# Scores in the up projection's two banks, six raw blocks ahead, embeddings later, and 256 instead of 512 tokens' down projection in float32

## The chip, the cores and the metric

The kernel runs on one core of a Trainium2 chip. The metric is the device time of one execution in microseconds; the median of three runs of the kernel before is 1092.6 us (1091.49 to 1093.6). Five engines work side by side, each through its own queue in order: PE (TensorE, matmuls), DVE (VectorE), ACT (ScalarE), POOL (GpSimd) and SP (SyncE, here the queue of most DMA issues).

## The reference

Three stages follow each other, on float64 inputs for w_in and w_out and float32 for most else:

```
attention, B=8 batches, H=8 heads, S=512 tokens, Ns=32 states, D=64:
  scores  = x @ state^T / 8 ; a = softmax(scores) ; xread = a @ state
  scores2 = state @ x^T / 8 ; a2 = softmax(scores2) ; sread = a2 @ x
  out = concat(xread, sread) -> 4608 tokens x 512
moe:   h = x @ w_in (512 x 2048) ; g = relu(h)^2 ; y = g @ w_out (2048 x 512)
moe2:  logits = normalize(y) @ normalize(expert_emb)^T / tau
       expert = argmax ; gate = softmax(logits)[expert], 8 experts
       out = gate * (relu(y @ w1[expert]) @ w2[expert])      (512 -> 1024 -> 512)
```

## The kernel before

The kernel is one program without loops on the chip. Python generators (`attention`, `block`, `up1`, `down1`, `embeddings`, ...) stand for threads of work; a `Plan` runs them against a clock of its own. Each `yield "engine", duration` asks for an engine, and the planner always issues the piece that can start first by its clock (`dep`, `free`), and among equals the one with the smaller priority number. A `yield ev(...)` waits for an event, a `yield slots` for a free buffer. What it issues in that order is each engine's queue on the chip, so the planner's durations set the order of work, not its time.

*Weights.* w_in and w_out are each read in eight raw blocks of 1 MB (i0 to i7 and o0 to o7, in the order i0 i1 o0 o1 i2 i3 ...). `weights()` asks for them one after another; `AHEAD` says from which block on it waits until both transposes of the first batch's attention weights have been asked for (events "asked"). A raw block becomes float32 in `to_f32` (an ACT conversion at L903, a cast at L910 on ACT or L913 on DVE, and an or on DVE at L916), is squared for its scale (L935 and L991 on ACT), and is later split into a high and a low float16 half: w_in in `wi_split` (L978), w_out in `wo_split` (L1039 on ACT, then DVE in `split_lo`, L317). The halves of w_out's block q go where the float32 copy of block q - 2 lies, so the split of block q waits for the float32 matmuls that read block q - 2: `yield ev("down32", F32U - 1, q - 2)`.

*Attention folded into the up projection.* The read xread @ w_in is computed as a @ (state @ w_in). For each batch, state @ w_in is made in four pieces k = 0 to 3 (events ("sw", b, k)): for the first batch in float32 from the float32 blocks of w_in (`first_state_w`, PE at L650, scaled and split at L660 and L317), for the others in float16. The S tile in PSUM (`ps_s`, two banks, one slot `s_slots`) holds these pieces, and also the scores of a batch.

*The first batch.* `first_attention` scores x in float32 in two halves t = 0, 1 (`first_scores`, L598); `weigher` makes the softmax (L520 maximum, L522 subtraction, L529 exponential, L531 sum, L537 division, L541 and L543 the two float16 halves) and asks for a transpose (L550). In the kernel before both halves lie in one S tile.

*Token groups.* The 4608 tokens are taken in groups u of 256, two groups a batch, u = 16 for all states. `up1` makes the hidden layer in eight chunks of 256 columns for each group (L1379 to L1381, three float16 matmuls for a product), `hidden` applies relu (L1332) and the square, and `down1` makes the output of each tile of 128 tokens. For the groups u < F32U the square stays float32 (L1336) and the down projection is done in float32 from the unsplit w_out (L1442). For the others the square is split in a high and a low half (L1344 or L1349, L1346, L1351) and the down projection takes three float16 matmuls (L1463 to L1465), which need the splits of w_out (`ev("wo", a)` in the first such group). With F32U = 2, `up1` alternates chunks of u = 0 and u = 1 as the pieces of state @ w_in come. From u = 2 on, chunk c of a group waits for part c - 1 of the down projection before it.

*Embeddings and constants.* `embeddings` loads the expert embeddings, tau and the float16 constants through ACT's DMA queue and normalizes the embeddings with 22 short DVE instructions (itau at L1166, the root at L308 to L314, the rest at L1183 to L1189) and four matmuls (L1174). `prepare` loads the other constants through SP and writes a row of records; its event "prepared" opens `down1`. The routing of each output tile (`route_tile`) waits for the embeddings (event "en").

Behind the first stage the experts' weights are converted, records of tokens are written to DRAM, and `moe2` works through lists of tokens by expert until the end.

Of the kernel before, what the change touches and what calls it, by code (L numbers as in the profile page):

```python
# [10 lines left out]
F32 = mybir.dt.float32  # L11
# [10 lines left out]
B, H, S, D, NS = 8, 8, 512, 64, 32  # L22
# [21 lines left out]
BLOCKS = [(kind, 2 * k + i) for k in range(NB // 2) for kind in "io" for i in range(2)]  # L44
RAW_IN = ('g0', 'g2', 'stage0', 'stage1', 'g1', 'g3', 'phl', 'wo8', 'stage0', 'stage1', 'phl', 'wo8', 'stage0', 'stage1',
          'phl', 'stage0')
F32U = 2
PRIO_W = 1
PRIO_SPLIT = 1.3
EASE = 1.0  # L50
LOADER = 9
AHEAD = 4
PRIO_A0 = 0.8
PRIO_A1 = 1.5
PRIO_S0 = 1.1
# [190 lines left out]
def moe_kernel(  # L246
# [17 lines left out]
    nc = tc.nc  # L264
    ctx.enter_context(tc.manual_schedule())
    plan = Plan()
# [70 lines left out]
    def load(dst, src, nbytes):  # L337
        yield "sp", 0.06
        nc.sync.dma_start(dst, src)
        return plan.dma(nbytes)  # L340
# [60 lines left out]
    def ev(*key):  # L401
        return evs.setdefault(key, Ev(plan))
# [46 lines left out]
    def attention(b):  # L449
# [50 lines left out]
        for sb in range(4):  # L500
            for c in range(4):
                o = Sp[:, sb, c * 64:c * 64 + 64]
                ss_ = slice(sb * 128, sb * 128 + 128)
                for n, (a, w) in enumerate(pairs):
                    mm(o, lhsT=w[:, c, ss_], rhs=a[:, c, :], start=n == 0, stop=n == 2)
        w = weigher(b, Sp, xh, xl, scl, 0, 32)
        yield from w

    def weigher(b, Sp, xh, xl, scl, m0, m1):

        ms, n = slice(m0, m1), NS * (m1 - m0)
        S4 = Sp.rearrange("p a (h n) -> p (a h) n", n=NS)[:, ms]
        mx = small.tile([128, 32], F32, name="mx")[:, ms]
        e1 = xh.rearrange("p c s -> p (c s)").bitcast(F32).rearrange("p (m n) -> p m n", n=NS)
        a16 = xl.rearrange("p c s -> p (c s)").rearrange("p (t c m n) -> p t m c n", t=2, c=4, n=NS)
# [5 lines left out]
        yield dve(n)  # L521
        V.tensor_tensor(out=e1, in0=S4, in1=mx.unsqueeze(2).to_broadcast([128, m1 - m0, NS]), op=ALU.subtract)  # L522
        ev("S read", b, m1).set()
        if m1 == 32:
            if m0:
                yield ev("S read", b, m0)
            s_slots.release()
        yield act(n)
        nc.scalar.activation(out=e1, in_=e1, func=AF.Exp, scale=scl)  # L529
        yield dve(n)  # L530
# [30 lines left out]
    def first_attention():  # L561

        yield ev("st", 0)
        stt = st_t.pop(0)
        yield xhl_slots
        xh, xl = halves_tile()
        ss = small.tile([128, 3], F32, name="ss")
        yield act(256)
        nc.scalar.activation(out=xl.bitcast(BF16)[:, :, :64], in_=stt, func=AF.Square, accum_out=ss[:, 2:3])
        yield t_slots  # L570
        p = ps_t.tile([128, 512], F32, name="t")
        yield "pe", 0.2
        mm(p[:, 2:3], lhsT=one32, rhs=ss[:, 2:3], start=True, stop=True)
        mm(p[:, 256:512], lhsT=oneb, rhs=xl.bitcast(BF16)[:, :, :64], start=True, stop=True)
        yield s_slots
        Sp = ps_s.tile([128, 4, 256], F32, name="S")
        for t in range(2):
            plan.add(first_scores(t, Sp, xh, xl, stt), 0.4 + 0.1 * t)
        plan.add(first_scale(ss, stt), 0.95)
        v = small.tile([128, 2], F32, name="sv")[:, 0:1]  # L580
        yield tiny(4)
        V.tensor_scalar(out=v, in0=p[:, 2:3], scalar1=FLOOR, scalar2=None, op0=ALU.max)
        pow2(sx[:, 1:2], isx[:, 1:2], v, 204)
        yield sth_slots
        sthl = att.tile([128, 2, 4, 64], F16, name="sthl")
        stf = sthl.rearrange("p a c n -> p (a c n)").bitcast(F32).rearrange("p (c n) -> p c n", c=4)
        yield dve2(256)
        V.tensor_scalar(out=stf, in0=stt, scalar1=sx[:, 1:2], scalar2=float(2.0 ** -14), op0=ALU.mult, op1=ALU.mult)
        plan.add(first_state_w(stf), 0.6)
        plan.add(group_bound(0, p), 0.7)  # L590

    def first_scores(t, Sp, xh, xl, stt):
        yield ev("first x", t)
        xf = xf_t[0, 0]
        yield "pe", 2.0
        for sb in (2 * t, 2 * t + 1):
            for c in range(4):
                mm(Sp[:, sb, c * 64:c * 64 + 64], lhsT=xf[:, c, sb * 128:sb * 128 + 128], rhs=stt[:, c, :],  # L598
                   start=True, stop=True)
        ev("scored", t).set()  # L600
        yield from weigher(0, Sp, xh, xl, eighth, 16 * t, 16 * t + 16)

    def first_scale(ss, stt):

# [551 lines left out]
        ev("experts").set()  # L1156

    def embeddings():
        yield "act", 1.0
        nc.scalar.dma_start(emf, embT)  # L1160
        nc.scalar.dma_start(tsb, tau.to_broadcast([128, 1]))
        nc.scalar.dma_start(cs16, cst16)
        plan.cur[2] += 2.5
        ev("identb").set()
        yield tiny(3)
        V.reciprocal(out=itau, in_=tsb)  # L1166
        V.tensor_scalar(out=itau, in0=itau, scalar1=float(2.0 ** -14), scalar2=None, op0=ALU.mult)
# [679 lines left out]
    def prepare():  # L1847

        yield ev("w_in asked")
        yield from load(cs, cst, 1 << 17)  # L1850
        yield from load(rid, rowid, 1 << 15)
        t = plan.now()
        yield "pool", 1.0, t + 2.0
        dz = mg.tile([128, REC], F32, name="rec0", bufs=1)
        nc.gpsimd.memset(dz, 0.0)
        nc.gpsimd.tensor_copy(dz[:, 513:514].bitcast(I32), rid[:, NT:NT + 1])
        yield from load(rec_d[NOREC:NOREC + 1, :], dz[0:1, :].bitcast(I32), 2048)
        ev("prepared").set()

    def start():  # L1860
        plan.add(first_attention(), PRIO_A0)
        yield from load_st(0)
        yield from load_x(0, 0)
        plan.add(embeddings(), 0.9)
        yield from block(0)
        plan.add(weights(), 1)
        for b in range(1, B):
            plan.add(attention(b), 1.15 if b == 1 else PRIO_A1)
        plan.add(loader(), 1)
        plan.add(prepare(), 1)  # L1870
        plan.add(up1(), 5)
        plan.add(down1(), 5)
        plan.add(moe2(0, NMAIN), 5)
        plan.add(switch(), 2.1)
# [46 lines left out]
```

## Time and profile before

| | us |
|---|---|
| median of 3 runs | 1092.6 |
| profiled execution | 1093.78 |
| its span, first to last instruction | 1091.6 |
| PE busy | 1041.7 |
| DVE busy | 665.7 |
| ACT busy | 591.4 |
| POOL busy | 127.4 |

The busy time of an engine is the time in which an instruction of it was running; the rest of the span it was idle. A row of an engine in order of time gives start and length, the line of the kernel, the operation, what it wrote from what it read, and in brackets how long the engine had been idle before and which instruction ended that.

### The profile page before, as it was taken

The page shows a single profiled execution, that of the slowest core. Times are in us where ns is not written, and L with a number is a line of the kernel's source. Part 1 is how long each engine was busy: PE and PEld are TensorE (multiplying, and loading weights), DVE is VectorE, ACT ScalarE, POOL GpSimd, SP SyncE. Part 2 cuts the span into 40 slices and gives each one's busy share as a digit, 9 for nine tenths or more (in the row PEclk, how much of TensorE's full clock was granted, in tenths as well). Part 3 has the DMA queues.
Part 4 walks back from the last instruction along what each step waited for, and adds up shares of the span by engine and source line. Part 5 has one row for each costly group of instructions (what it writes and reads, how often), then busy time and mean ns, then how long its engine had stood idle before and what let it go on. Part 6 is the DMA issues. An engine that isn't in the chain of part 4 may idle for free. (4 is left out here: it accounts for less than half of the span.)

```text
span 1091.6 us, 26343 instructions
## 1 busy us (share of the span) xinstructions
PE 1041.7 (95%) x10657; PEld 672.5 (62%) x10657; DVE 665.7 (61%) x1766; ACT 591.4 (54%) x981; POOL 127.4 (12%) x149
## 2 busy tenths in 40 slices
PE   4799999998999999999999999899999999999998
PEld 3454455665566566555665666476767777767674
DVE  5877878778887798787877764465322222222222
ACT  4899886988898878788778684111111010111110
POOL 0000002001002002010020100312112121212101
PEclk9799999999999999999999999999999999999999
DMA  6883384656767648757768477944896666694591
GB/s 210 305 273 121 59 228 138 171 187 154 223 172 241 218 102 228 208 130 222 180 193 233 124 244 237 255 99 106 276 293 177 182 205 213 185 270 145 166 313 72
DMA packets 161311, 211.74 MB, mean 194 GB/s; under 512 B 112225, under 2 KB 115041, under 8 KB 155938
## 3 DMA queue, kind: packets, MB, share of 16 engines
q1 hardware_dynamic: 152434, 182.86, 58.2%
q0 software_dynamic: 8320, 27.08, 7.7%
q8 instruction: 85, 1.39, 0.5%
q14 instruction: 40, 0.33, 0.1%
q10 hardware_dynamic: 432, 0.08, 0.0%
HBM read 257.92 MB, written 51.68 MB: 284 GB/s over the span
## 5 line engine op out<-in xcount | busy, mean ns | idle before, releaser
L1729 ACT ACTIVATE r<-u 128x512 f32<-128x512 f32 x70 | 41.8, 597 | 326.8 <-PE u L1775 308.4
L1463 PE MATMUL d<-wo_t,g 128*128 128x512 f16 x480 | 182.6, 380 | 0.7 <-DVE f L1207 0.7
L1464 PE MATMUL d<-wo_t,g 128*128 128x512 f16 x480 | 182.7, 381 | 0.0
L1465 PE MATMUL d<-wo_t,g 128*128 128x512 f16 x480 | 182.5, 380 | 0.1
L1379 PE MATMUL u<-aT,sw 128*128 128x256 f16 x512 | 140.7, 275 | 6.2 <-ACT r L1332 4.9
L1381 PE MATMUL u<-aT,sw 128*128 128x256 f16 x512 | 140.6, 275 | 0.3 <-issue 0.3
L1380 PE MATMUL u<-aT,sw 128*128 128x256 f16 x512 | 140.6, 275 | 0.0
L1732 DVE CAST hh<-r 128x512 f16<-128x512 f32 x70 | 30.0, 429 | 140.2 <-ACT r L1729 138.7
L1332 ACT ACTIVATE r<-u,cg 128x512 f32<-128x512 f32 x120 | 81.8, 683 | 47.2 <-PE u L1381 27.3
L1305 POOL DMA_INDIRECT rec_d<-rec,pi x34 | 39.0, 1147 | 486.4 <-DVE rec L1301 120.0
L1743 DVE TENSOR_SCALAR o<-d,rec,wo_t 128x512 f32<-128x512 f32 x35 | 28.3, 810 | 104.9 <-PE d L1798 104.9
L1798 PEld LDWEIGHTS <-hh 128*128 128x128 f16 (+1 forms) x688 | 54.6, 102 | 56.5 <-issue 0.4
L1351 DVE TENSOR_TENSOR g<-r,g 128x512 f16<-128x512 f32 x120 | 82.4, 688 | 8.1 <-ACT r L1346 5.3
L1465 PEld LDWEIGHTS <-g 128*128 128x128 f16 x480 | 47.1, 98 | 57.6 <-issue 0.8
L1773 PE MATMUL u<-xes,stage 128*128 128x128 f16 x448 | 76.0, 219 | 0.2 <-issue 0.2
L1774 PE MATMUL u<-xes,stage 128*128 128x128 f16 x448 | 76.0, 219 | 0.0
L1775 PE MATMUL u<-xes,stage 128*128 128x128 f16 x448 | 76.0, 219 | 0.0
L1346 ACT ACTIVATE r<-r 128x512 f32<-128x512 f32 x120 | 74.6, 627 | 1.4
L1463 PEld LDWEIGHTS <-g 128*128 128x128 f16 x480 | 47.5, 99 | 44.5 <-issue 0.5
L1464 PEld LDWEIGHTS <-g 128*128 128x128 f16 x480 | 47.1, 98 | 45.0 <-issue 1.4
L1774 PE MATMUL u<-xes,xx 128*128 128x128 f16 x416 | 70.4, 219 | 0.4 <-issue 0.4
L1773 PE MATMUL u<-xes,xx 128*128 128x128 f16 x416 | 70.5, 219 | 0.1
(330 smaller groups left out, 2620.4 us busy)
## 6 DMA issues: line engine op xcount, KB each, us to landing
w_d<-he SPq DMA_DIRECT2D x128, 256.0 KB
g<-w_d SPq DMA_DIRECT2D x16, 2048.0 KB
wo_t<-w_d SPq DMA_DIRECT2D x16, 2048.0 KB
stage<-w_d SPq DMA_DIRECT2D x14, 2048.0 KB
he<-w_d SPq DMA_DIRECT2D x14, 2048.0 KB
xx<-w_d SPq DMA_DIRECT2D x13, 2048.0 KB
sw<-w_d SPq DMA_DIRECT2D x13, 2048.0 KB
stage<-in_w_dram SPq DMA_DIRECT2D x20, 1024.0 KB
```

Source lines behind the costliest of these rows:

```text
L1332: nc.scalar.activation(out=r, in_=ps, func=AF.Relu, scale=cg[:, g:g + 1] if u >= F32U else cgq[:, c:c + 1])
L1346: nc.scalar.activation(out=r, in_=r, func=AF.Square)
L1351: V.tensor_tensor(out=gl, in0=r, in1=gh, op=ALU.subtract)
L1379: mm(o, lhsT=hl[:, i, 0, fs], rhs=aT[:, i, :], start=i == 0, stop=False)
L1380: mm(o, lhsT=hl[:, i, 0, fs], rhs=aT[:, 2 + i, :], start=False, stop=False)
L1381: mm(o, lhsT=hl[:, i, 1, fs], rhs=aT[:, i, :], start=False, stop=i == 1)
L1463: mm(ps, lhsT=g_h[:, f, ts], rhs=w[:, 0, :], start=f == 0, stop=False)
L1464: mm(ps, lhsT=g_h[:, f, ts], rhs=w[:, 1, :], start=False, stop=False)
L1465: mm(ps, lhsT=g_l[:, f, ts], rhs=w[:, 0, :], start=False, stop=f == KF - 1)
L1773: mm(p[:, j, xs], lhsT=w[:, 0, k, fs], rhs=xe[:, k, xs], start=k == 0, stop=False)
L1774: mm(p[:, j, xs], lhsT=w[:, 0, k, fs], rhs=xe[:, 4 + k, xs], start=False, stop=False)
L1775: mm(p[:, j, xs], lhsT=w[:, 1, k, fs], rhs=xe[:, k, xs], start=False, stop=k == 3)
```

## The change

Five edits, made together:

- the two halves of the first batch's scores go to two tiles of the up projection's pool (`ps_u`, one bank each) instead of one S tile, and each gives its slot back after its own subtraction; the planner books 3.4 instead of 2.0 us of PE for a half;
- `AHEAD` is 6 instead of 4;
- `embeddings` no longer loads anything and starts behind "prepared" at priority 3 (0.9 before);
- its three loads are issued through SP in `prepare`, and the row of records is booked behind the last of them;
- `F32U` is 1 instead of 2.

```diff
--- before.py
+++ after.py
@@ -44,12 +44,12 @@
 BLOCKS = [(kind, 2 * k + i) for k in range(NB // 2) for kind in "io" for i in range(2)]
 RAW_IN = ('g0', 'g2', 'stage0', 'stage1', 'g1', 'g3', 'phl', 'wo8', 'stage0', 'stage1', 'phl', 'wo8', 'stage0', 'stage1',
           'phl', 'stage0')
-F32U = 2
+F32U = 1
 PRIO_W = 1
 PRIO_SPLIT = 1.3
 EASE = 1.0
 LOADER = 9
-AHEAD = 4
+AHEAD = 6
 PRIO_A0 = 0.8
 PRIO_A1 = 1.5
 PRIO_S0 = 1.1
@@ -503,13 +503,12 @@
                 ss_ = slice(sb * 128, sb * 128 + 128)
                 for n, (a, w) in enumerate(pairs):
                     mm(o, lhsT=w[:, c, ss_], rhs=a[:, c, :], start=n == 0, stop=n == 2)
-        w = weigher(b, Sp, xh, xl, scl, 0, 32)
+        w = weigher(b, Sp.rearrange("p a (h n) -> p (a h) n", n=NS), xh, xl, scl, 0, 32, s_slots.release)
         yield from w
 
-    def weigher(b, Sp, xh, xl, scl, m0, m1):
+    def weigher(b, S4, xh, xl, scl, m0, m1, read):
 
         ms, n = slice(m0, m1), NS * (m1 - m0)
-        S4 = Sp.rearrange("p a (h n) -> p (a h) n", n=NS)[:, ms]
         mx = small.tile([128, 32], F32, name="mx")[:, ms]
         e1 = xh.rearrange("p c s -> p (c s)").bitcast(F32).rearrange("p (m n) -> p m n", n=NS)
         a16 = xl.rearrange("p c s -> p (c s)").rearrange("p (t c m n) -> p t m c n", t=2, c=4, n=NS)
@@ -521,10 +520,7 @@
         yield dve(n)
         V.tensor_tensor(out=e1, in0=S4, in1=mx.unsqueeze(2).to_broadcast([128, m1 - m0, NS]), op=ALU.subtract)
         ev("S read", b, m1).set()
-        if m1 == 32:
-            if m0:
-                yield ev("S read", b, m0)
-            s_slots.release()
+        read()
         yield act(n)
         nc.scalar.activation(out=e1, in_=e1, func=AF.Exp, scale=scl)
         yield dve(n)
@@ -572,10 +568,8 @@
         yield "pe", 0.2
         mm(p[:, 2:3], lhsT=one32, rhs=ss[:, 2:3], start=True, stop=True)
         mm(p[:, 256:512], lhsT=oneb, rhs=xl.bitcast(BF16)[:, :, :64], start=True, stop=True)
-        yield s_slots
-        Sp = ps_s.tile([128, 4, 256], F32, name="S")
         for t in range(2):
-            plan.add(first_scores(t, Sp, xh, xl, stt), 0.4 + 0.1 * t)
+            plan.add(first_scores(t, xh, xl, stt), 0.4 + 0.1 * t)
         plan.add(first_scale(ss, stt), 0.95)
         v = small.tile([128, 2], F32, name="sv")[:, 0:1]
         yield tiny(4)
@@ -589,16 +583,22 @@
         plan.add(first_state_w(stf), 0.6)
         plan.add(group_bound(0, p), 0.7)
 
-    def first_scores(t, Sp, xh, xl, stt):
+    def first_scores(t, xh, xl, stt):
         yield ev("first x", t)
         xf = xf_t[0, 0]
-        yield "pe", 2.0
-        for sb in (2 * t, 2 * t + 1):
+        at = plan.now()
+        yield u_slots
+        plan.cur[2] = max(at, plan.now())
+        Sp, k_h = ps_u.tile([128, 512], F32, name="u").rearrange("p (a n) -> p a n", a=2), u_slots.last()
+        yield "pe", 3.4
+        for a in range(2):
+            sb = 2 * t + a
             for c in range(4):
-                mm(Sp[:, sb, c * 64:c * 64 + 64], lhsT=xf[:, c, sb * 128:sb * 128 + 128], rhs=stt[:, c, :],
+                mm(Sp[:, a, c * 64:c * 64 + 64], lhsT=xf[:, c, sb * 128:sb * 128 + 128], rhs=stt[:, c, :],
                    start=True, stop=True)
         ev("scored", t).set()
-        yield from weigher(0, Sp, xh, xl, eighth, 16 * t, 16 * t + 16)
+        yield from weigher(0, Sp.rearrange("p a (h n) -> p (a h) n", n=NS), xh, xl, eighth, 16 * t, 16 * t + 16,
+                           lambda: u_slots.release(k_h))
 
     def first_scale(ss, stt):
 
@@ -1156,12 +1156,7 @@
         ev("experts").set()
 
     def embeddings():
-        yield "act", 1.0
-        nc.scalar.dma_start(emf, embT)
-        nc.scalar.dma_start(tsb, tau.to_broadcast([128, 1]))
-        nc.scalar.dma_start(cs16, cst16)
-        plan.cur[2] += 2.5
-        ev("identb").set()
+        yield ev("prepared")
         yield tiny(3)
         V.reciprocal(out=itau, in_=tsb)
         V.tensor_scalar(out=itau, in0=itau, scalar1=float(2.0 ** -14), scalar2=None, op0=ALU.mult)
@@ -1848,9 +1843,11 @@
 
         yield ev("w_in asked")
         yield from load(cs, cst, 1 << 17)
+        yield from load(cs16, cst16, 1 << 16)
         yield from load(rid, rowid, 1 << 15)
-        t = plan.now()
-        yield "pool", 1.0, t + 2.0
+        yield from load(tsb, tau.to_broadcast([128, 1]), 512)
+        t = yield from load(emf, embT, 1 << 14)
+        yield "pool", 1.0, t
         dz = mg.tile([128, REC], F32, name="rec0", bufs=1)
         nc.gpsimd.memset(dz, 0.0)
         nc.gpsimd.tensor_copy(dz[:, 513:514].bitcast(I32), rid[:, NT:NT + 1])
@@ -1861,13 +1858,13 @@
         plan.add(first_attention(), PRIO_A0)
         yield from load_st(0)
         yield from load_x(0, 0)
-        plan.add(embeddings(), 0.9)
         yield from block(0)
         plan.add(weights(), 1)
         for b in range(1, B):
             plan.add(attention(b), 1.15 if b == 1 else PRIO_A1)
         plan.add(loader(), 1)
         plan.add(prepare(), 1)
+        plan.add(embeddings(), 3)
         plan.add(up1(), 5)
         plan.add(down1(), 5)
         plan.add(moe2(0, NMAIN), 5)
```

## Rows read from the trace of the kernel before

**Rows 1.** The page, part 1: busy time, share of the span, instructions
```profile
PE 1041.7 (95%) x10657; PEld 672.5 (62%) x10657; DVE 665.7 (61%) x1766; ACT 591.4 (54%) x981; POOL 127.4 (12%) x149
```

**Rows 2.** Windows: length, each engine's busy time, TensorE's clock, DMA share, GB/s
```profile
0.00:28.00 28.00, 12.77 (x51) 9.91 (x51) 15.68 (x54) 13.94 (x19) 1.23 (x10) 0.89 0.64 210
28.00:91.30 63.30, 54.74 (x415) 31.60 (x416) 49.40 (x101) 59.31 (x88) 3.57 (x7) 0.89 0.76 267
91.30:151.60 60.30, 55.71 (x415) 29.80 (x414) 47.57 (x101) 50.82 (x83) 0.00 (x0) 1.00 0.47 131
151.60:1091.60 940.00, 918.52 (x9780) 601.20 (x9777) 553.10 (x1515) 467.29 (x794) 122.62 (x132) 1.00 0.67 193
```

**Rows 3.** PE in order of time: start, length, line, tiles, count, [idle before]
```profile
6.98 7.06 PE L598 MATMUL S<-stt,xx 128*128 128x64 f32 x32 [2.09 <-DMA xx<-in_xT_dram]
...
28.04 1.11 PE L650 MATMUL S<-wi,sthl 64*32 64x256 f32 x16 [9.09 <-DVE wi L916]
...
46.52 3.60 PE L1442 MATMUL d<-wo_t,g 128*128 128x512 f32 x8
49.96 0.27 PE L1379 MATMUL u<-aT,sw 128*128 128x256 f16 x1
...
151.61 0.38 PE L1463 MATMUL d<-wo_t,g 128*128 128x512 f16 x1
...
154.20 0.17 PE L1226 MATMUL t<-en_h,xr 128*128 128x8 f16 x1
```

**Rows 4.** DVE in order of time, same columns
```profile
14.08 0.69 DVE L520 TENSOR_REDUCE mx<-S 128x16 f32<-128x512 f32 x1 [6.40 <-PE S L598]
...
16.73 0.16 DVE L308 TENSOR_SCALAR rst<-env 128x8 int32<-128x8 int32 x1
...
18.82 1.27 DVE L531 TENSOR_REDUCE sm<-xx 128x16 f32<-128x512 f32 x2
...
25.55 2.35 DVE L916 SCALAR_TENSOR_TENSOR wi<-g,wi 128x1024 int32<-128x1024 int32 x2
...
90.59 0.75 DVE L317 SCALAR_TENSOR_TENSOR sw<-S,swi,sw 128x512 f16<-128x512 f32 x1 [0.41 <-ACT sw L660]
...
136.28 1.28 DVE L317 SCALAR_TENSOR_TENSOR wo_t<-wo_t,swo 128x1024 f16<-128x1024 f32 x1
```

**Rows 5.** ACT in order of time, same columns
```profile
8.59 1.06 ACT L613 ACTIVATE pjk<-xx 128x1024 bf16<-128x1024 f32 x1 [4.64 <-DMA xx<-in_xT_dram]
...
15.59 0.72 ACT L529 ACTIVATE xx<-xx,eighth 128x512 f32<-128x512 f32 x1 [5.85 <-DVE xx L522]
...
17.87 2.11 ACT L903 ACTIVATE rec<-g 128x1024 f16<-128x1024 bf16 x2
```

**Rows 6.** SP's DMA issues in order of time, same columns
```profile
24.45 2.75 SPq L550 DMA_TRANSPOSE aT<-xx  x2
27.25 1.17 SPq L339 DMA_DIRECT2D g<-in_w_in_dram  x2
```

**Rows 7.** Windows of the start, columns of Rows 2
```profile
13.00:14.00 1.00, 1.00 (x6) 1.00 (x6) 0.00 (x0) 0.00 (x0) 0.00 (x0) 1.00 1.02 403
18.00:25.20 7.20, 0.95 (x4) 0.00 (x0) 6.72 (x25) 6.25 (x7) 0.00 (x0) 0.77 0.01 3
20.00:30.00 10.00, 1.96 (x20) 0.69 (x20) 9.29 (x23) 7.40 (x8) 0.00 (x0) 0.60 0.40 74
```

**Rows 8.** Groups by line, first 165 us: count | busy us, mean ns | idle before
```profile
L1332 ACT ACTIVATE r<-u,cgq 128x512 f32<-128x512 f32 x16 | 10.9, 683 | 0.8 <-PE u L1381 0.6
L1336 ACT ACTIVATE g<-r 128x512 f32<-128x512 f32 x16 | 10.0, 626 | 0.0
L1039 ACT ACTIVATE wo_t<-wo_t,swo 128x1024 f16<-128x1024 f32 x8 | 9.1, 1143 | 1.7 <-PE d L1442 1.7
...
L1351 DVE TENSOR_TENSOR g<-r,g 128x512 f16<-128x512 f32 x6 | 4.0, 684 | 0.0
L1349 DVE CAST g<-r 128x512 f16<-128x512 f32 x6 | 2.5, 423 | 0.7 <-ACT r L1346 0.4
```

## The prediction

> **What bounds the kernel now.** I read the page's busy times first, then windows of the whole run, and then PE, DVE, ACT and SP in order of time through the start. The busy times show TensorE at 1041.7 us of a span of 1091.6 [rows 1]: it is the bound, and 49.9 us are idle. The windows place the idle time: 15.2 us before 28.0 us, 8.6 us up to 91.3 us and 4.6 us up to 151.6 us, 28.4 us in all; the other 21.5 us are spread over the 940 us behind [rows 2]. So this kernel can get shorter in two ways: less work on PE, or less idle time in the first 151.6 us. In the middle stretch ACT is busy 59.31 of 63.3 us, DVE 49.40 [rows 2]: while the weights are taken apart, ACT paces PE.
>
> The start itself is a chain. PE scores the first batch from 6.98 to 14.04 us, later waits 9.09 us, and takes its first weight piece at 28.04 us [rows 3]. DVE waits for the last of the scores, starts at 14.08 us, and from there has no gap until the conversion of the two blocks that PE waits for, which begins at 25.55 us and takes 2.35 us [rows 4]. ACT sits idle 5.85 us until DVE gives it the first subtracted scores at 15.59 us; the raw blocks behind that instruction are converted only from 17.87 us [rows 5]. The DMA engines meanwhile have nothing to do between 18 and 25.2 us (share 0.01) [rows 7], because SP stands at the transposes of the weights of attention, issued at 24.45 us, and the next raw block is asked for at 27.25 us [rows 6].
>
> The profiled execution took 1093.78 us, 2.18 us more than its span and 1.2 us more than the median of 1092.6. I work on the span and take both off at the end.
>
> **The change part by part.**
>
> *256 tokens fewer in float32.* A float32 matmul leaves two records; eight records take 49.96 - 46.52 = 3.44 us, 0.43 us each [rows 3]. Group u = 1 has two token tiles of 16 blocks, so 64 records: 64 x 0.43 = 27.5 us go. In float16 the same blocks cost three matmuls each, 2 x 16 x 3 = 96; twelve stand from 151.61 to 154.20 us, 0.216 us each [rows 3], so 20.7 us come. PE saves 6.8 us, and since PE is dense behind the start, I count all of it.
> What it costs elsewhere: hidden(u = 1) keeps its two ACT passes (683 and 626 ns) and gains a cast and a subtraction on DVE, 423 + 684 ns [rows 8], eight times: 8.9 us of DVE. PE hides them if DVE isn't late for the splits of w_out. And the down projection of u = 1 now needs those splits, as that of u = 2 did.
>
> *The order of up1.* With one float32 group, chunks of u = 1 no longer alternate with those of u = 0; they follow all eight. Up to six of them (three of four weight pieces) leave the stretch before the last piece, which DVE finishes at 91.3 us [rows 4]. They take 6 x 12 matmuls of 256 columns from PE, half of 0.216 us each, 7.8 us, and on ACT 6 x 1.31 = 7.8 us [rows 8]. ACT being 94% busy there [rows 2], the last piece comes between 0 and 7.8 us sooner; I take 5.5, nearer the upper end as ACT has so little slack.
>
> *Scores in two banks.* Each half of the scores has a tile of its own, so the first reduction can follow its own 16 records: at 6.98 + 3.5 = 10.5 us instead of 14.08 us [rows 3, 4]. It also leaves the S tile free for the first weight piece. The planner books 3.4 instead of 2.0 us for a half, which places the exponentials behind the conversion of block 0 on ACT. Block 0 can be there early: x has landed by 8.59 us [rows 5] and a block of 1.05 MB at 403 GB/s [rows 7] takes 2.6 us, so block 0 comes at about 11.2 and block 1 at 13.8 us (estimates from these rows).
>
> *Embeddings later.* Eleven short DVE instructions stand from 16.73 to 18.82 us [rows 4], 0.19 each; with the seven that follow the reductions that is 18 x 0.19 = 3.4 us, out of a stretch in which DVE has no gap. They come back behind "prepared" at priority 3, where DVE has 14 us of gaps in 63 [rows 2]: I count them as hidden there, at 3.4 us if they aren't. Three DMA issues leave ACT's queue and go to SP's, behind the constants; they delay SP by at most three of the 0.6 us that g's issues take (1.17 us for two) [rows 6], and push nothing that PE waits for.
>
> *Six raw blocks ahead.* Blocks 4 and 5 are issued before SP waits for the transposes, in the 7.2 us in which DMA idles [rows 7]; by 2.6 us a block they land at about 21.5 and 24.1 us, against an issue at 27.25 us before [rows 6]. The transposes stand behind them in the queue: at worst 5.2 us later, and they aren't needed before the first up projection.
>
> *Together, at the start.* Block 1 at 13.8 us, one conversion (half of 2.11) [rows 5], a cast and an or of half of 2.35 us [rows 4], and some 2 us behind score work give a first weight piece at about 19 us instead of 28.04: 9 us, between 4 (if DVE's order keeps all the score work ahead) and 11. ACT then has its work moved up by at most the idle time that it gets rid of, 5.85 us before the exponentials [rows 5] and some of its other gaps; of the 9 us I let 7 pass on and take 1 us off for embeddings and constants.
> So the last weight piece of batch 0 comes at 91.3 - 7 - 5.5 + 1, about 80 us. By then PE has done 12.8 + 54.7 - 7.8 = 59.7 us of work. What it can do without a split of w_out is the 123.2 us done by 151.6 us [rows 2] less 27.5 of float32 and about 6 of u = 2: 90 us. So 30 us are left at 80 us; with 5 us of stalls (the handover of the two output tiles, a first split) it is through at 115 us, with 25 us idle instead of 28.4.
>
> *The sum.* Span: 115 + (1041.7 - 6.8 - 90) + 21.5 = 1081.4 us, that is 6.8 us of work and 3.4 us of idle time less. With 2.2 us around it and 1.2 us down to the median: **1082.5 us**.
>
> *The splits as the check on this.* The second tile pass of u = 1 can't start its last quarter before the last split of w_out, which ends at 137.6 us now [rows 4]. By the end of its first tile PE has 90 + 10.4 + about 6.5 (five chunks of u = 2), 107 us of work behind it, so a last split at W gives a span of W + 2.6 + (1034.9 - 107) + 21.5 = W + 952. From 91.3 to 137.6 are 46.3 us, of which DVE idles about a fifth (47.57 of 60.3 busy) [rows 2]; the work, 36.5 us, plus 8.9 makes 45.4 us. From 80 us that is W = 125 to 128: 1077 to 1080, so the splits don't decide, but by a few us only.
>
> **The rivals.**
>
> *The start's gain doesn't arrive.* ACT's order, not the data, may set the pace: its 59.31 of 63.3 us [rows 2] leave 4 us to win, and only 1.31 us a chunk is taken out. Then the last piece comes at 91.3 - 5.5 + 1.5 = 87.3 us, PE is through at 122.3 us, and the median is about 1089.5. For it: saturation. Against it: three idle places of the start that lie on the chain.
>
> *The splits become the wait (slower).* If the last weight piece stays near 91.3 us and DVE's 8.9 us come on top, W = 91.3 + 46.3 + 8.9 = 146.5, the span 1098.5 and the median about 1099.5. The place is the down projection of u = 1, where 27.5 us of float32 matmuls used to cover the splits; it decides from W = 139.6 on, where the span is what it was. For it: the cover is gone, and u = 2's chunks are paced by this down projection. Against it: ACT's first passes of the splits waited 1.7 us for these very matmuls [rows 8], as each split overwrites what they read, and that wait goes.
>
> *TensorE's clock.* With fewer chunks in it, the stretch from 19 to 80 us holds 54.7 - 7.8 = 47 us of PE work at a granted clock of 0.89 [rows 2]. From 20 to 30 us, when PE was busy 1.96 us, it was granted 0.60, between its two levels of 1.2 and 2.4 GHz [rows 7]. At 0.60 all along, 47 us become 70 in a stretch of 61: 9 us late, a median of about 1091.5, no change; at 1.2 GHz throughout it would be 84 us and a clear loss. It decides from about 0.69 down. Against it: 28 to 91.3 us held 0.89 with gaps. The Trainium skill, "TensorE: Matmul & The Clock Gate", part 1, speaks against the change here: it calls half rate the default and has activity release it, and idling return it. The drop in the window from 20 to 30 us agrees; taken alone, the rule gives this rival's time.
>
> **How the numbers follow.** The forecast has 0.54, with a range of its own from 1075 (all 9 us of the start arrive) to 1089. The lost start has 0.17 (1089.5, two thirds of it still faster), the splits 0.18 (1092 to 1100, mostly slower), the clock 0.11 (spread over all three). A difference of 0.2%, 2.2 us, is about what a measurement here can tell. Faster: 0.54 + 0.11 + 0.03 = 0.68; same: 0.06 + 0.03 + 0.05 = 0.14; slower: 0.15 + 0.03 = 0.18. The range runs from 1074 to 1097: it leaves out the far end of the splits' case and a start that loses still more idle time.
>
> **What would show it.** Right: L1442 has 64 records; the first reduction of scores starts near 10.6 us; the first weight piece on PE (L650) near 19 us; the last split of w_out ends before 130 us; PE's idle time up to the dense part falls to about 25 us; the 940 us behind keep their 21 us. Wrong: L650 not before 24 us, PE waiting on w_out's splits (L1463) for more than 5 us, a granted clock under 0.69 from 20 to 80 us, or new waits for the embeddings (en) in the first routing.

## The result and the profile after

The changed kernel takes 1100.6 us in the median of five runs (1098.52 to 1104.42), the kernel before 1093.32 us in the same comparison: a ratio of 1.0068 (95%: 1.0043 to 1.0092), slower, where 1082.5 us were forecast. The profiled execution is the slowest of the five: 1104.42 us, span 1102.6. The account below is of this execution, and so explains 11.0 us where the medians differ by 7.3.

The page, part 1, of the kernel after (answers [rows 1]):

```profile
PE 1043.5 (95%) x10689; PEld 673.9 (61%) x10689; DVE 669.0 (61%) x1773; ACT 594.9 (54%) x988; POOL 127.3 (12%) x149
```

PE should be busy 6.8 us less, and is busy 1.8 us more: at half clock a matmul is busy for longer (rows below: 0.42 us instead of 0.27). So both times have to be taken apart by stretch. Columns as in [rows 2]. Kernel before, then after: start, middle, the hand-over from the first stage to the experts, and the rest:

```profile
0.00:150.00 150.00, 121.92 (x867) 70.14 (x868) 111.29 (x250) 122.48 (x185) 4.79 (x17) 0.93 0.62 203
150.00:690.00 540.00, 532.06 (x4550) 321.19 (x4550) 421.22 (x1160) 424.68 (x721) 47.54 (x60) 1.00 0.67 188
690.00:730.00 40.00, 36.09 (x399) 25.06 (x398) 19.96 (x93) 5.99 (x12) 6.46 (x8) 0.96 0.81 206
730.00:1091.60 361.60, 351.67 (x4845) 256.12 (x4843) 113.28 (x266) 38.22 (x64) 68.62 (x65) 1.00 0.66 198
```

```profile
0.00:150.00 150.00, 124.67 (x926) 71.09 (x927) 119.44 (x268) 131.89 (x201) 6.54 (x17) 0.89 0.65 209
150.00:690.00 540.00, 527.90 (x4518) 318.33 (x4517) 420.65 (x1179) 418.98 (x714) 44.83 (x59) 1.00 0.65 185
690.00:730.00 40.00, 28.74 (x286) 20.54 (x285) 13.42 (x64) 4.57 (x10) 7.83 (x9) 0.83 0.80 205
730.00:1102.60 372.60, 362.24 (x4965) 263.94 (x4963) 115.47 (x264) 39.43 (x66) 68.06 (x65) 1.00 0.65 194
```

Idle time of PE is length less busy time. I call clock loss the busy time times (1 - granted clock), added up over stretches of 1 us; what is left of PE's busy time is work at full clock. For all kernels, from one profiled execution each (idle + clock loss, us):

| kernel | span | work | start, 0-150 | middle, 150-690 | hand-over, 690-730 | rest |
|---|---|---|---|---|---|---|
| before | 1091.6 | 1034.1 | 28.1 + 6.0 | 7.9 + 0 | 3.9 + 1.7 | 9.9 |
| after | 1102.6 | 1027.7 | 25.3 + 12.8 | 12.1 + 0 | 11.2 + 3.1 | 10.3 |
| a1_f32u1 | 1104.4 | 1031.1 | 36.9 + 8.5 | 11.7 + 2.9 | 1.3 + 0 | 11.9 |
| r1_f32u2 | 1098.4 | 1034.0 | 27.4 + 9.0 | 13.2 + 1.5 | 2.9 + 0 | 10.3 |
| r2_embearly | 1105.5 | 1032.9 | 28.6 + 2.6 | 14.6 + 1.7 | 10.5 + 3.7 | 10.9 |
| r3_ahead4 | 1091.9 | 1025.7 | 28.8 + 7.7 | 13.6 + 4.1 | 2.3 + 0 | 9.7 |
| m3_skip | 1088.8 | 1026.5 | 29.2 + 8.7 | 12.0 + 1.4 | 0 + 0.3 | 10.6 |
| m2_hold | 1087.8 | 1027.6 | 28.6 + 5.4 | 9.6 + 0 | 4.1 + 2.5 | 10.0 |
| m1_warm | 1096.2 | 1040.3 | 18.5 + 4.6 | 11.0 + 0 | 8.0 + 2.0 | 11.7 |
| e1_prio | 1089.1 | 1027.1 | 29.8 + 5.9 | 13.4 + 1.7 | 0.3 + 0 | 10.7 |
| e2_warm_prio | 1093.4 | 1038.7 | 20.2 + 5.1 | 12.4 + 3.4 | 2.6 + 0 | 11.0 |
| e0_prio | 1095.7 | 1034.6 | 27.8 + 6.1 | 10.6 + 0 | 3.3 + 2.3 | 10.9 |
| p1_tiny | 1111.1 | 1037.4 | 30.2 + 6.6 | 14.6 + 1.7 | 6.1 + 4.7 | 10.0 |
| p2_marg | 1088.3 | 1035.9 | 27.8 + 3.9 | 10.7 + 0 | 0 + 0 | 10.0 |

The work term holds to some 3 us only: before, r1, e0, p1 and p2 have the same matmuls and lie between 1034.0 and 1037.4. After less before: work -6.4, start +4.0, middle +4.2, hand-over +8.7, rest +0.4, together +10.9 of the 11.0 us.

Each row of the table is one execution, and executions of one program differ. m2, m3 and e1, described below, issue the same work in the same order as after on PE, DVE and ACT up to 580 us, and e0 the same as before up to 575 us. Idle time and clock loss of PE up to 575 us:

| order of before | order of after |
|---|---|
| before 40.8, e0 40.7 | after 48.7, m3 47.5, e1 44.7, m2 41.9 |

So up to 7 us of the 8.2 lost in start and middle may belong to this one execution; what the change itself costs there lies between 1 and 8 us. The hand-over doesn't rest on the table alone: the medians of the experiments below repeat it.

**The start.** PE after, in order of time (columns of [rows 3]):

```profile
5.51 7.06 PE L597 MATMUL u<-stt,xx 128*128 128x64 f32 x32 [1.13 <-DMA xx<-in_xT_dram]
17.16 0.66 PE L650 MATMUL S<-wi,sthl 64*32 64x256 f32 x16
21.07 1.11 PE L650 MATMUL S<-wi,sthl 64*32 64x256 f32 x16 [3.25 <-DVE wi L916]
28.10 0.40 PE L1374 MATMUL u<-aT,sw 128*128 128x256 f16 x1 [4.14 <-ACT sw L660]
...
32.41 0.42 PE L1374 MATMUL u<-aT,sw 128*128 128x256 f16 x1
32.62 0.42 PE L1375 MATMUL u<-aT,sw 128*128 128x256 f16 x1
...
37.09 0.27 PE L1375 MATMUL u<-aT,sw 128*128 128x256 f16 x1
37.20 0.27 PE L1376 MATMUL u<-aT,sw 128*128 128x256 f16 x1
```

DVE after (answers [rows 4]):

```profile
9.19 0.69 DVE L519 TENSOR_REDUCE mx<-u 128x16 f32<-128x512 f32 x1 [2.38 <-PE u L597]
...
80.58 0.75 DVE L317 SCALAR_TENSOR_TENSOR sw<-S,swi,sw 128x512 f16<-128x512 f32 x1 [0.76 <-ACT sw L660]
...
122.02 2.47 DVE L317 SCALAR_TENSOR_TENSOR wo_t<-wo_t,swo 128x1024 f16<-128x1024 f32 x2
```

The first weight piece is on PE at 17.16 instead of 28.04 us; the last one leaves DVE at 81.3 instead of 91.3, the last split of w_out at 124.5 instead of 137.6. But the second piece waits 3.25 us for its block, the first up projection 4.14 us for ACT, and matmuls of 256 columns follow each other every 0.21 us at 32.4 us and every 0.11 us at 37.1 us: half clock, then full. Windows after, by clock:

```profile
12.00:20.00 8.00, 5.37 (x31) 1.72 (x30) 7.86 (x18) 7.94 (x12) 0.00 (x0) 0.98 1.03 401
20.00:36.00 16.00, 9.15 (x75) 4.33 (x76) 12.87 (x26) 15.97 (x22) 0.00 (x0) 0.50 0.93 293
...
41.00:47.00 6.00, 5.82 (x17) 2.91 (x15) 5.71 (x10) 6.00 (x10) 0.18 (x1) 0.50 0.93 363
...
81.00:88.00 7.00, 6.17 (x30) 4.50 (x31) 6.15 (x17) 5.94 (x10) 0.00 (x0) 0.51 0.65 265
```

The early start is a sparse one: 5.37 us of work in 8, then 16 us at 0.50 (1.2 GHz), in which ACT has no gap (15.97 of 16). The Trainium skill, "TensorE: Matmul & The Clock Gate", part 1, has idling return the clock to half rate; the stretch from 20 us on agrees. How much half clock follows differs between executions of the same order. Two of these windows in m2:

```profile
20.00:36.00 16.00, 9.34 (x84) 5.02 (x85) 12.89 (x27) 15.97 (x23) 0.00 (x0) 0.57 0.93 300
...
81.00:88.00 7.00, 7.00 (x43) 4.28 (x41) 6.79 (x17) 6.82 (x10) 0.00 (x0) 1.00 0.61 219
```

From 20 to 36 us all four executions of this order were granted 0.50 to 0.57. From 41 to 47 us it was 0.50 to 1.00, from 81 to 88 us 0.51 to 1.00. The clock loss of their first 150 us runs from 5.4 (m2) to 12.8 us (after).

**The hand-over.** PE after, around the end of the first stage:

```profile
699.22 0.38 PE L1460 MATMUL d<-wo_t,g 128*128 128x512 f16 x1
707.07 0.19 PE L1221 MATMUL t<-en_h,xr 128*128 128x8 f16 x1 [7.47 <-DMA xr<-rec]
...
710.26 0.27 PE L1768 MATMUL u<-xes,stage 128*128 128x128 f16 x1 [2.71 <-DMA xes<-rec]
```

The last down projection is done, and PE stands for the last tile's transposed record (xr, for its routing), then for the first transposed list of expert tokens (xes). SP's issues before, then after, show what went ahead of these transposes:

```profile
656.22 10.17 SPq L339 DMA_DIRECT2D w_d<-he  x8
668.41 0.37 SPq L1679 DMA_DIRECT2D stage<-w_d  x1
670.50 0.34 SPq L1679 DMA_DIRECT2D he<-w_d  x1
...
687.50 3.11 SPq L1719 DMA_TRANSPOSE xes<-rec  x2
693.45 1.24 SPq L1217 DMA_TRANSPOSE xr<-rec  x1
696.72 0.35 SPq L1679 DMA_DIRECT2D xx<-w_d  x1
```

```profile
670.18 5.57 SPq L339 DMA_DIRECT2D w_d<-he  x6
677.93 0.36 SPq L1674 DMA_DIRECT2D stage<-w_d  x1
680.00 0.34 SPq L1674 DMA_DIRECT2D he<-w_d  x1
681.85 0.34 SPq L1674 DMA_DIRECT2D xx<-w_d  x1
692.28 2.76 SPq L1212 DMA_TRANSPOSE xr<-rec  x1
695.24 6.82 SPq L1714 DMA_TRANSPOSE xes<-rec  x1
```

L339 (`w_d<-he`) writes the experts' split weights to DRAM, L1674 (L1679 before) loads 2 MB of them for the expert stage. After the change the last write is issued at 675.4 instead of 666.1 us, and three loads, not two, go out ahead of both transposes. The DMA windows 690 to 700 us, before and after:

```profile
690.00:700.00 10.00, 6.48 (x50) 3.59 (x48) 4.94 (x29) 0.92 (x2) 1.52 (x3) 1.00 1.22 189
```

```profile
690.00:700.00 10.00, 9.60 (x45) 4.13 (x43) 1.27 (x5) 1.02 (x3) 6.43 (x7) 1.00 1.01 332
```

332 instead of 189 GB/s move while xr's transpose is on its way. Issued at 692.28 us it frees PE at 707.07, 14.8 us later; before, 693.45 to 700.18, 6.7 us. The queue of SP's transfers (q1) after, from 679 to 697 us and from 697.1 to 707 us: packets, MB, share:

```profile
q1 hardware_dynamic: 421, 6.16, 86.2%
...
q1 hardware_dynamic: 1714, 0.45, 41.2%
```

Up to 697 us it moves the three loads (packets of 16 KB for the most part), and only then the small packets (256 bytes) of the transposes, 4.8 us after xr's was issued. Before, the last packet of the two loads ends at 680.7 us, well ahead of xr's transpose.

### The profile page after: what moved, and what is told of

It is laid out like the page before. It is cut to its first block, busy times and chain, and to the rows that moved or that the text cites. A ratio compares the mean times of both kernels' runs of the same rounds, so it can differ in the third digit from the quotient of the medians.

```text
span 1102.6 us, 26389 instructions
## 1 busy us (share of the span) xinstructions
PE 1043.5 (95%) x10689; PEld 673.9 (61%) x10689; DVE 669.0 (61%) x1773; ACT 594.9 (54%) x988; POOL 127.3 (12%) x149
## 5 line engine op out<-in xcount | busy, mean ns | idle before, releaser
L1459 PE MATMUL d<-wo_t,g 128*128 128x512 f16 x512 | 194.3, 379 | 2.8 <-DVE wo_t L317 2.8
L1458 PE MATMUL d<-wo_t,g 128*128 128x512 f16 x512 | 194.2, 379 | 1.6 <-DVE g L1344 1.0
L1460 PE MATMUL d<-wo_t,g 128*128 128x512 f16 x512 | 194.3, 379 | 0.5 <-issue 0.4
L1374 PE MATMUL u<-aT,sw 128*128 128x256 f16 x512 | 142.5, 278 | 15.5 <-ACT sw L660 8.3
L1376 PE MATMUL u<-aT,sw 128*128 128x256 f16 x512 | 142.4, 278 | 0.7 <-DVE sw L317 0.7
L1375 PE MATMUL u<-aT,sw 128*128 128x256 f16 x512 | 142.4, 278 | 0.0
L1327 ACT ACTIVATE r<-u,cg 128x512 f32<-128x512 f32 x128 | 87.4, 683 | 53.3 <-PE u L1376 34.4
L1346 DVE TENSOR_TENSOR g<-r,g 128x512 f16<-128x512 f32 x128 | 87.8, 688 | 6.9 <-ACT r L1341 5.4
L1460 PEld LDWEIGHTS <-g 128*128 128x128 f16 x512 | 50.1, 98 | 64.3 <-issue 3.9
L1768 PE MATMUL u<-xes,stage 128*128 128x128 f16 x448 | 78.4, 223 | 2.7 <-DMA xes<-rec 2.7
L1341 ACT ACTIVATE r<-r 128x512 f32<-128x512 f32 x128 | 80.0, 627 | 1.4
L1458 PEld LDWEIGHTS <-g 128*128 128x128 f16 x512 | 50.3, 98 | 49.5 <-DVE g L1344 1.5
L1459 PEld LDWEIGHTS <-g 128*128 128x128 f16 x512 | 50.0, 98 | 47.9 <-issue 1.1
L1769 PE MATMUL u<-xes,stage 128*128 128x128 f16 x448 | 78.4, 223 | 0.0
L1770 PE MATMUL u<-xes,stage 128*128 128x128 f16 x448 | 78.3, 223 | 0.0
L1374 PEld LDWEIGHTS <-sw 128*128 128x128 f16 x512 | 52.2, 102 | 36.4 <-issue 15.3
L1768 PE MATMUL u<-xes,xx 128*128 128x128 f16 x416 | 70.5, 219 | 0.0
```

What stands on the lines that cost most here:

```text
L1327: nc.scalar.activation(out=r, in_=ps, func=AF.Relu, scale=cg[:, g:g + 1] if u >= F32U else cgq[:, c:c + 1])
L1341: nc.scalar.activation(out=r, in_=r, func=AF.Square)
L1346: V.tensor_tensor(out=gl, in0=r, in1=gh, op=ALU.subtract)
L1374: mm(o, lhsT=hl[:, i, 0, fs], rhs=aT[:, i, :], start=i == 0, stop=False)
L1375: mm(o, lhsT=hl[:, i, 0, fs], rhs=aT[:, 2 + i, :], start=False, stop=False)
L1376: mm(o, lhsT=hl[:, i, 1, fs], rhs=aT[:, i, :], start=False, stop=i == 1)
```

## The experiments

Three theories stood against each other. A: the loss is the hand-over, the experts' weights come late against the first stage. B: it is the clock of a sparser start. C: any edit draws another order from the planner, and the order before was a good one. All ratios are to the kernel before, with 95% intervals. Differences in us to the kernel after are those of medians.

**One edit alone, or all but one.** a1 is the kernel before with F32U = 1 only; r1, r2 and r3 are the changed kernel with one edit undone.

```diff
a1  (before) -F32U = 2          +F32U = 1
r1  (after)  -F32U = 1          +F32U = 2
r2  (after)  embeddings, their loads and prepare as in the kernel before
r3  (after)  -AHEAD = 6         +AHEAD = 4
```

> The kernel before with F32U = 1 alone. Theory A (the float32 edit pays for itself in TensorE time, and what is lost is lost at the hand-over to the last stage, where the experts' weights come late): PE work falls by 6.8 us, but with nothing to fill the first 90 us at least 5 us are lost to a lower granted clock and to waits; ratio 0.997 to 1.005, and slower only if the last experts' piece is written later than 665 us. Theory B (the sparse start is the loss: fewer PE instructions in it, half clock): slower by 0.5% or more, clock loss (busy time times one minus the granted clock) in the first 150 us above 10 us, against 6.0 us before.

Measured: 1105.91 us, 1.0104 (1.0068 to 1.014). Slower, as B has it, but its clock loss in the start is 8.5, not above 10. The last write comes late, at 684.5 us, but the hand-over costs 1.3 us only: neither theory has the place.

> The changed kernel with F32U = 2 again, so the three edits of the start alone. Theory A: the start comes 9 us earlier, and the time depends on whether the experts' weights come earlier too: last piece written by 658 us gives ratio 0.992, 672 us or later gives 1.003 or more. Theory B: with the float32 chunks back as filler the clock loss falls to 7 us or less and the whole gain of the start arrives: ratio 0.990 to 0.994 whatever the experts do.

Measured: 1105.71 us, 1.0099 (1.0068 to 1.0131); the profiled execution took 1100.58 us. The last write comes at 674.8 us, for which A has 1.003 or more, but the hand-over costs only 2.9 us. B's gain isn't there.

> The changed kernel with the embeddings where they were (own loads on ACT's queue, priority 0.9). Both theories: 3.4 us of short DVE instructions are back in the start, the first weight piece on PE comes some 2 us later, the time moves by less than 0.3% if the order of work behind stays the same. If the time moves by more than 0.5%, it is through the order of the whole program behind it (Theory C: any edit reshuffles the planner's order, and the hand-over to the last stage falls well or badly by it).

Measured: 1102.83 us, 1.0091 (1.0061 to 1.0122), 2.2 us above after, within the 0.3%; but the first weight piece comes 8.2 us later, not 2.

> The changed kernel with AHEAD = 4. Blocks 4 and 5 are asked for behind the transposes again, some 4 us later. Theory A and B: second weight piece up to 4 us later, time within 0.3% of the changed kernel. Theory C: a shift of either sign by more than 0.5%, with the last experts' piece and the idle time at the hand-over (690 to 720 us) moving along with it.

Measured: 1095.08 us, 1.0011 (0.9991 to 1.0032), 5.5 us below after; the last write comes at 661.1 us. A and B had no change; C had this.

What follows: no single edit carries the loss, and no undoing brings back the forecast. F32U = 1 alone loses its float32 gain in the start (34.1 to 45.4 us of idle and clock); that the long matmuls had filled PE's gaps there is a reading, not shown. The start edits without it (r1) leave the start at 36.4, no better than before; with it (after) they take 7 us off a1's. AHEAD = 4 brings the hand-over down from 14.3 to 2.3 us, although it is an edit of the first 30 us. So the place of a loss need not be the place of the edit.

**The clock alone.** m1 adds matmuls of 256 columns, overwritten afterwards, in PE's gaps; the order of all other work is that of after. The trace has 104 of them (10793 records on PE, 10689 after), 11 of them ahead of the one sum for w_out's scale; the 209 and the second 11 in the text below are a miscount.

```diff
+    def warm(o, n):
+        for _ in range(n):
+            mm(o, lhsT=oneb, rhs=oneb.unsqueeze(1).to_broadcast([128, 2, 128]), start=True, stop=True)
...
+                if k == 0 and j == 1:
+                    warm(Sp[:, 0, 1, :], 24)
...
+        if acc is woacc:
+            warm(p[:, 256:512], 11)
...
+                    if u == 0 and ff == 0 and c in (0, 2, 6):
+                        warm(o, {0: 34, 2: 24, 6: 11}[c])
```

> The changed kernel with its order of work untouched, plus 209 float16-rate matmuls of 256 columns whose results are overwritten, put in four places where PE stood idle: 24 ahead of the second weight piece, 34, 24 and 11 ahead of up-projection chunks 0, 2 and 6 of the first group, and 11 and 11 ahead of the sums for the scales. Clock theory (B): the granted clock stays up, the clock loss of the first 150 us falls from 12.8 to 6 us or less, and the time falls by 4 to 7 us. If the half clock before 47 us is hidden, since ACT paces PE there, only the 3.1 us lost in the dense stretch from 82 to 88 us come back: 2 to 4 us. Hand-over theory (A): at most 3 us, and the idle time from 690 to 730 us stays at 10 us or grows by what the first stage gains.

Measured: 1098.07 us, 1.0044 (1.0027 to 1.0061). A window of m1, in which the executions without added matmuls were granted 0.50 to 0.57:

```profile
20.00:36.00 16.00, 13.27 (x128) 9.09 (x126) 14.00 (x31) 15.95 (x21) 0.00 (x0) 0.86 0.95 280
```

The time falls by 2.5 us, which fits the hidden clock (2 to 4) and A's "at most 3" alike. The clock loss of the start is 4.6 us, against 12.8 in the one execution of after; but m2, m3 and e1, in the same order and without added matmuls, have 5.4, 8.7 and 5.9, so most of that fall can be chance. ACT has no gap in this window in either kernel (15.95 and 15.97 of 16). Idle and clock loss of the start are 15.0 us below after's, and the work term is 12.6 higher: what the clock took had mostly been waiting time, now filled with added matmuls. What a faster clock would give that costs no such work isn't shown; B has at most these 2.5 us for it.

**The experts' weights.** m3 leaves out a part of the computation: the second matrix of the last expert is neither loaded nor converted; the one of the expert before is written twice. m2 keeps all work and holds back one of the expert stage's early loads, the third of those above, until the first stage's event "moe1".

```diff
m3  -for n in range(4 * NE):           +for n in range(4 * NE - 2):
    -for i in range(2 * NE):           +for i in range(2 * NE - 1):
m2  -yield ev("moe1") if name == "w2" else ev("cum", NXT - 1)
    +yield ev("moe1")
```

> The changed kernel without the load and conversion of the last expert's second matrix (it gets the sixth's, written twice), so the experts' weights are all written some 10 to 20 us sooner at the same order of work before that. Theory A: the 10 us of idle time between the stages fall to 3 us or less and the time falls by 6 to 9 us. Theory B: no more than 2 us, since the start is untouched.

Measured: 1090.65 us, 0.9975 (0.9949 to 1.0001).

> The changed kernel with the first weights of the second step (2 MB) loaded only when the first down projection is done, as the kernel before has it by chance. If the loss at the hand-over is the collision of three 2 MB loads with the records and transposes that PE waits for, the rest behind the last matmul of the first down projection falls from 404 to 390 to 396 us, and the time by 6 to 12 us. If it is the late end of the conversions by itself (first load, records, transposes, each in its turn), less than 3 us.

Measured: 1094.34 us, 1.0005 (0.9982 to 1.0027); the profiled execution took 1089.58 us, 4.8 less than the median. PE's longest wait for a transfer in its hand-over, and SP there:

```profile
PE u L1768 <- DMA xes<-rec: 4.1, 1, 4.1
```

```profile
673.52 0.34 SPq L1674 DMA_DIRECT2D he<-w_d  x1
685.31 2.66 SPq L1714 DMA_TRANSPOSE xes<-rec  x1
688.02 1.80 SPq L1212 DMA_TRANSPOSE xr<-rec  x1
689.88 3.32 SPq L1714 DMA_TRANSPOSE xes<-rec  x1
694.82 0.35 SPq L1674 DMA_DIRECT2D xx<-w_d  x1
```

The third load now stands behind the transposes, the wait for xr is gone, and with it 6.3 us of the changed kernel's median. m3 takes 10 us off it, though what it leaves out is next to no work of PE (2 of 10689 records): its last write is out at 659.2 us, its hand-over costs 0.3. Both speak for A. m2 says more: its writes end as late against the other work as those of after, and only the third load has moved.

All fourteen executions fall into two kinds. Where the last write is issued 30 us or more ahead of the last matmul of the first stage's down projection, the program takes 386 to 391 us from that matmul to its end. In after, m1 and r2 it is issued 22 to 24 us ahead, and the rest takes 400 to 403 us.

**The repair, and its controls.** PRIO_E1 is the priority of the experts' conversion once attention is through; a smaller number lets it go ahead of other work.

```diff
e1  (after)  -PRIO_E1 = 2.2     +PRIO_E1 = 1.9
e2  (m1)     -PRIO_E1 = 2.2     +PRIO_E1 = 1.9
e0  (before) -PRIO_E1 = 2.2     +PRIO_E1 = 1.9
p1  (before) -TINY = 0.18       +TINY = 0.19
p2  (before) -MARG = 1.75       +MARG = 1.7
```

> The changed kernel with the experts' conversions one step earlier in the planner's choice once attention is done (PRIO_E1 1.9 instead of 2.2), nothing else. Hand-over theory: the runs so far fall into two kinds by the time from the last write of the experts' weights to the last matmul of the first down projection: with 30 us or more (the kernel before 39, three others) the rest of the program takes 388 to 392 us from that matmul, with 26 us or less (the changed kernel, two others) 401 to 404. Here the last write comes 15 to 20 us earlier, so the rest takes 388 to 391 us and the time is 1086 to 1090, ratio 0.994 to 0.998. Clock theory alone: within 2 us of the changed kernel, 1098 to 1102.

Measured: 1090.92 us, 0.9976 (0.9954 to 0.9997), 9.7 us below the changed kernel; the rest takes 389.1 us. SP and the hand-over of e1:

```profile
644.92 9.67 SPq L339 DMA_DIRECT2D w_d<-he  x8
656.75 0.36 SPq L1674 DMA_DIRECT2D stage<-w_d  x1
...
678.42 0.35 SPq L1674 DMA_DIRECT2D xx<-w_d  x1
692.60 1.23 SPq L1212 DMA_TRANSPOSE xr<-rec  x1
```

```profile
690.00:730.00 40.00, 39.66 (x450) 28.38 (x449) 23.07 (x111) 6.24 (x13) 10.21 (x12) 1.00 0.71 170
```

The last write comes 21 us sooner than after (654.3 us), the third load is out 14 us before the transpose of xr, not 10, and PE idles 0.3 us instead of 11.2.

> Both repairs on the changed kernel: the overwritten matmuls that keep TensorE's clock up in the start, and PRIO_E1 1.9. If the two losses are separate they add: another 2 to 4 us below the run with PRIO_E1 alone, 1083 to 1087, ratio 0.991 to 0.995. If the second repair already takes back all (the early clock is hidden behind ACT), the two are the same within 1.5 us.

Measured: 1093.87 us, 0.9999 (0.9971 to 1.0027): neither of the two forecasts, but 2.95 us above e1, with intervals that overlap. So the added matmuls give no gain on top of e1 that these runs can tell.

> Control: the kernel before with PRIO_E1 1.9. Its experts' weights are in time already (39 us ahead), so the hand-over theory expects no gain there: ratio 0.998 to 1.004, with the rest behind the last matmul of the first down projection at 387 to 390 us as before. A gain of 0.5% or more would mean that the constant helps by something else, and that its effect on the changed kernel doesn't show the hand-over.

Measured: 1097.44 us, 1.0033 (1.0011 to 1.0056): the same constant makes the kernel before slower. So its gain on the changed kernel isn't a gain in general: what it repairs is the change's own loss.

> The kernel before with one constant of the planner changed (0.19 instead of 0.18 us booked for a short DVE instruction): the same work, another order from the start on. Theory C (the order of the kernel before is an unusually good draw, and any reshuffling costs some us in the middle and at the hand-over): 1.003 to 1.012 of the time before, idle time of 150 to 690 us above 10 us against 7.9. Theories A and B: within 0.3%.

Measured: 1117.45 us, 1.023 (1.0183 to 1.0277).

> The kernel before with the planner's margin for matmuls at 1.7 instead of 1.75 us: the same work and the same start (PE's order changes only behind the first 7% of its instructions). Theory C: 1.003 to 1.012 of the time before. Theories A and B: within 0.3%.

Measured: 1089.82 us, 0.9977 (0.9955 to 0.9998).

p1 and p2 have the work of the kernel before, in an order drawn from a planner constant that is 6% or 3% off: +25 and -2.5 us by their ratios. Neither lies in C's range, and p2 is where A and B had it. So the order before wasn't an unusually good one; but C holds in that an order alone is worth as much as the whole change. p1 loses 10.8 us from 690 to 730 us, p2 nothing; p1's is not the loss of after, as only 2.8 us of it are a wait for xr and its rest takes 391 us.

## Why the prediction was wrong

*The work* came out: 64 float32 records are left of 128, and PE's work at full clock falls by 6.4 us, against 6.8 forecast (within the 3 us that such a number holds to); in m2, m3 and e1 it is 6.5 to 7.6 us below before.

*The data's path through the start* came out too: the first reduction at 9.19 us (forecast 10.6, its matmuls started 1.5 us sooner), the first piece at 17.16 (19), the last one at 81.3 (80), the last split at 124.5 (125 to 128). The splits didn't become the wait: L1459 waited for them 2.8 us in all. Nor did the embeddings: they are ready at 68.4 us, and the first routing is at 104.9.

*"25 us idle instead of 28.4"* failed, though this execution has 25.3. That number is luck: the step took the matmuls at the durations of before, and here waiting became slow matmuls, so that idle plus clock loss rose from 34.1 to 38.1 us. m2, m3 and e1, in the same order, have 28.6 to 29.8 us idle and 34.0 to 37.9 in sum; r1 and r3 have 36.4 and 36.5. In none of them did the start get shorter than before, though PE takes its first weight piece 10 to 11 us sooner. Only r2, with the embeddings early, has less, 31.2, and its work term is 5.2 us above that of after, more than that term's uncertainty; so whether the later embeddings cost the start something stays open.

This is what the first rival came to, a gain that doesn't arrive, but not its way: it put the last piece at 87.3 us, and that came at 81.3, as forecast. Its reason, ACT, is in the rows: ACT is busy 15.97 of 16 us, and PE waits 8.3 us in three waits for ACT's scaling of the pieces (L660). That it is the whole reason isn't shown. The clock rival went part of its way: 0.80 from 19 to 80 us, above its point of 0.69; the 7 us more at half rate from 81 us on are this execution's, and m2 and e1 don't have them.

*"I count all of it"* and the term of 21.5 us behind the start failed. The sum let every microsecond won in the first stage reach the end. With the clock loss, as in the table, the stretches behind 150 us cost 23.4 us before and 36.7 after; 8.7 of the 13.3 are the hand-over, which no step and no rival looked at. What ends there is a race of two chains: the first stage's last tiles, and the conversion of the experts' weights on engines that aren't PE, through SP and DRAM. [rows 2] showed only 940 us in one window, with 21.5 us of idle time to treat as a constant; a window of 40 us at the stage's end would have shown the 3.7 us that PE waited for xr already. Its price is shown by e1 (9.7 us), m3 (10.0) and m2 (6.3), with the control e0 in the other direction. That is about the whole 7.3 us by which the medians differ.

*The middle* gives the remaining 4.2 us of these two executions. PE waits longer for relu there; its longest group of waits from 150 to 690 us, before, after and in m2:

```profile
PE u L1379 <- ACT r L1332: 3.7, 6, 1.7
```

```profile
PE u L1374 <- ACT r L1327: 5.9, 10, 1.0
```

```profile
PE u L1374 <- ACT r L1327: 4.7, 8, 1.0
```

From 150 to 575 us PE is idle for 6.8 us before and 6.7 in e0, for 10.7 after, and for 7.9, 9.6 and 8.9 in m2, m3 and e1, which have after's order there. So the new order costs 1 to 4 us in this stretch, and part of the 4.2 is the one execution's own. A run that repairs this alone was not made, and which of its waits are to blame stays open.

*What is left.* e1 gains 7.0 us of work and has 4.4 us more idle time than before (profiles), at the same clock loss: -2.6 us, as its ratio says. Against the forecast of 1082.5 us, 8.4 us are still missing: by the table its start is 5.0 us above what was forecast (3.4 less than before) and its middle 7.2, of which 5.1 behind 575 us, where its order is its own, while its hand-over gives back 5.3 that the forecast hadn't counted. e1 beats both kernels, but by no more than p2, which has no change in its work.

## What to carry to other kernels

Where a static order joins two stages, a gain in the first is only worth what the second can take up: window the last 40 us of each stage, and write down by how much the next stage's first inputs are early, before counting a gain through to the end. Count idle time and clock loss together, as a slow clock hides waits inside busy time (38.1 us in the start here, of which 25.3 show as idle). Before explaining a difference of two profiles, look at a second execution of the same order: here two differ by 7 us up to 575 us. And where a planner sets the order, run the old work in one or two other orders first: here that spread, -2.5 to +25 us, is larger than the change.

## What the runs showed of the hardware

A DMA transpose stood behind 2 MB loads issued earlier on the same queue: its small packets began only when those of the loads ended, 4.8 us after its issue. From issue to use it took 14.8 us with three loads ahead, the last of them 10 us earlier, and 6.7 us with two, the last 23 us earlier. TensorE's granted clock differs between executions of one order of work: 0.51 to 1.00 from 81 to 88 us, and 5.4 to 12.8 us of clock loss in the first 150. With 104 matmuls added in the gaps it was 0.86 instead of 0.50 to 0.57 from 20 to 36 us, and the kernel gained 2.5 us, where another engine set the pace.
